# Retention and a bilinear feed-forward on one core: state sums on GpSimd and out of PSUM, marks on ScalarE

## The chip, the cores and the metric

The kernel runs on one core of a Trainium2 chip. A core has TensorE (PE, matrix products into PSUM), VectorE (DVE), ScalarE (ACT), GpSimd (POOL) and SyncE (SP), which here only issues DMAs. Each engine works its own list of instructions in order, and waits where an instruction needs something that another engine or a DMA has yet to deliver. The metric is the time of one execution on the device in microseconds (us); lower is better.

## The reference

```python
gamma = 1.0 - 2.0 ** (-5.0 - np.arange(H))          # B, H, S, D = 4, 8, 768, 64
for t in range(S):
    state = gamma * state + einsum('bhd,bhe->bhde', k[:, :, t], v[:, :, t])
    y[:, :, t] = einsum('bhd,bhde->bhe', q[:, :, t], state) / sqrt(D)
x = y.transpose(0, 2, 1, 3).reshape(B * S, H * D)   # 3072 x 512
out = ((x @ w_a) * (x @ w_b)) @ w_out               # 512 -> 1536 -> 512
```

Inputs and output are float32.

## The kernel before

**Retention.** The 3072 positions are cut into 24 *slots* of 128, six to a batch. The decay is folded into tables that multiply k and q, so a chunk needs scores, a mask and a running state without decay. Slots are worked in *pairs*: pair n is slots n and n + 1. For each slot `casts(t)` (L243) puts on GpSimd two multiplies (`scaled`, L236: k and q by their tables, f32 to bf16, tile kqb) and the cast of v (`cast`, L201, tile vb), and on SyncE the DMA transpose of kqb to kqT (L249). After an odd slot it also issues the loads of the next pair (k, q, then v). So the chain casts, transpose, loads, casts of the next pair runs by itself, as far as buffers allow.

**A visit.** `turn(new, old)` (L407) is called at fixed places, and I name a visit by its arguments: visit 10/8 is `turn(10, 8)`. On TensorE it issues, in this order: the first half of the old pair's products with the state (`inter`, swapped, L369), the new pair's four chunk states in 64 rows (`chunk_states`, L292, two PSUM tiles named st), the new pair's scores (L327), the second half of `inter`, and the products of masked scores with v (`intra`, L381). Between the two halves the rows of a PSUM bank change; a tiny copy, the *mark* (`fenced`, L346), waits for the first half, and the second half waits for the mark.

A state at a chunk's end is the sum of all chunk states up to there. ScalarE copies the two st tiles into the SBUF tile sums (L298); each chunk is then added to the one before it (L303, VectorE, 128x256 f32, both inputs in SBUF), and ScalarE casts the sums to bf16, two at a time (gst, L199), for the next visit's `inter`. The adds are not run at the visit: they go on a list, `unsummed`, and `sum_now` takes one from it in each block of the feed-forward, or all of them behind an output.

**Feed-forward.** The positions form eight *tiles* J of TILES[J] slots (4, 2, 2, 2, 2, 4, 4, 4). Each tile runs twelve *blocks* (`ffn_ab`, L617): a (four matmuls, L594), ScalarE's cast of a to asb (L598), g (four matmuls, L606), VectorE's product of g and asb into ht (L609). In the tiles of FAST, VectorE also adds parts of ht into hsum (L665), and the output is computed for two slots at once by a scheme with seven products in place of eight (`ffn_fast`, L678): ScalarE copies product tiles to snap (L687), VectorE adds snap and PSUM into osb. The products into R1 and R5 go on accumulating after a snap has been taken, so TensorE waits for those copies. The other tiles use `ffn_out` (L632, L642).

**Order.** Each engine's order is the order of the code (`seq`). The dictionary `ahead` (L840) says what runs ahead of which block or output: `(5, 8)` is ahead of block 8 of tile 5, `(5, "o", 2)` ahead of output 2 of tile 5. Small ScalarE work goes on the list `later`: the copies of y to xt, and the casts to gst. `catch_up(n)` takes n from it; a block takes TILES[J] // 2, an `ffn_fast` takes two after its first snap and then one at a time.

The PSUM pool psff is a ring of three banks ("ff"), shared by a, g, o, one of the two st tiles and the fast products. The nat pool holds kqb and vb of six slots, the raw pool the loads of three pairs.

Of the kernel before, what the change touches and what calls it, by code (L numbers as in the profile page):

```python
# [12 lines left out]
ALU = mybir.AluOpType  # L13
# [11 lines left out]
def kernel(  # L25
# [10 lines left out]
    nc = tc.nc  # L36
    P = 128
    B, H, S, D = q.shape
    NCH = S // P
# [32 lines left out]
    def seq(bi):  # L72
        ins = bi.ins
        prev = last.get(ins.engine)
        if prev is not None:
            tc.add_manual_dep(ins, prev.name, nosync, reason="program order")
        last[ins.engine] = ins
        return bi
# [89 lines left out]
    for par in range(2):  # L168
        m = const.tile([P, 1, P], BF16, name=f"mask{par}")
# [8 lines left out]
    gst = const.tile([P, 8, HP, D], BF16, name="gst")  # L178
# [18 lines left out]
    def cast(engine, dst, src):  # L197
        if engine is nc.scalar:
            seq(nc.scalar.copy(dst, src))  # L199
        else:  # L200
            seq(engine.tensor_copy(dst, src))  # L201
# [57 lines left out]
    def half(i):  # L259
        return slice(64 * i, 64 * i + 64)  # L260
# [4 lines left out]
    later = []  # L265

    def catch_up(n=100):
        for fn in later[:n]:
            fn()
        del later[:n]  # L270

    sums = {}

    unsummed = []

    def sum_now(n=100):
        for fn in unsummed[:n]:
            fn()
        del unsummed[:n]

    def chunk_states(n):

        u = [psff.tile([P, 2, HP, D], F32, tag="ff", name="st"),
             psst.tile([P, 2, HP, D], F32, tag="st", name="st")]
        ends = (n + 2) % NCH == 0
        for s in range(2):
            for hp in range(HP):
                for c in range(2):
                    if ends and s and c:
                        continue  # L290
                    for r in range(2):
                        seq(nc.tensor.matmul(u[c][half(r), s, hp, :], kb[n + s][half(c), hp, r, :],  # L292
                                             vb[n + s][half(c), HP * r + hp, :],
                                             start=True, stop=True, skip_group_check=True))
        new = sums[n] = tra.tile([P, 2, 2, HP, D], F32, tag="kqT2", name="sums", bufs=2)
        for c in range(2):
            m = 1 if ends and c else 2
            seq(nc.scalar.copy(new[:, :m, c], u[c][:, :m]))  # L298

        def add_state(s, c):  # L300
            if s or c or n % NCH:
                old = new[:, s, 0] if c else new[:, 0, 1] if s else sums[n - 2][:, 1, 1]
                seq(nc.vector.tensor_tensor(new[:, s, c], new[:, s, c], old, op=ALU.add))  # L303
            m = 1 if ends and s else 2
            if c == m - 1:
                i = (2 * (n + s)) % 8
                later.append(lambda: cast(nc.scalar, gst[:, i : i + m], new[:, s, :m]))

        for s in range(2):
            for c in range(2):  # L310
                if not (ends and s and c):
                    unsummed.append(lambda s=s, c=c: add_state(s, c))

    unmasked = []

    def mask_now(n=100):
        for fn in unmasked[:n]:
            fn()
        del unmasked[:n]

    def scores(n):
        at = psat.tile([P, 2, 2, HP, D], F32, tag="at", name="at")
        for s in range(2):
            for hp in range(HP):
                for c in range(2):
                    for r in range(2):
                        seq(nc.tensor.matmul(at[half(c), r, s, hp, :],  # L327
                                             kqT[n + s][half(r), 0, hp, half(c)],
                                             queries(n + s, r, hp, c),
                                             start=True, stop=True, skip_group_check=True))  # L330
        aT[n] = tra.tile([P, 2, 2, HP, D], BF16, tag="aT", name="aT")
        for r in range(2):
            unmasked.append(lambda r=r: seq(nc.vector.tensor_tensor(  # L333
                aT[n][:, r].rearrange("p s h d -> p (s h) d"),
                at[:, r].rearrange("p s h d -> p (s h) d"),
                mask.to_broadcast([P, 2 * HP, D]), op=ALU.mult)))
# [7 lines left out]
    def fenced(eng):  # L344

        bi = seq(eng.copy(mark, bq) if eng is nc.scalar else eng.tensor_copy(mark, bq))  # L346
        tc.add_manual_dep(bi.ins, last[mybir.EngineType.PE].name, after, reason="rows change banks")
        return bi.ins
# [10 lines left out]
    def inter(o, swap, y):  # L359

        for s in range(2):
            for j in range(2):
                for r in range(2):
                    c = 1 - r if swap else r
                    t = o + s
                    if t % NCH == 0 and c == 0:
                        continue
                    for hp in (2 * j, 2 * j + 1):
                        into(o, c, r, seq(nc.tensor.matmul(  # L369
                            y[c][half(hp % 2), s, 2 * r + j, :], gst[half(r), (2 * t + c - 1) % 8, hp, :],  # L370
                            queries(t, r, hp, c), stop=y is not ys[o],
                            start=y is not ys[o] or begin(o, c, hp % 2),
                            skip_group_check=True)))
# [29 lines left out]
                seq(nc.vector.tensor_tensor(dst[:, s, on], src[:, s, on], part[:, s], op=ALU.add))  # L403
                seq(nc.vector.tensor_copy(dst[:, s, off], src[:, s, off]))

    def turn(new, old, eng=nc.vector):
        sum_now()  # L407
        catch_up()
        apart = None
        if old is not None:  # L410
            ys[old] = [psat.tile([P, 2, KT, D], F32, tag=f"y{c}", name="y") for c in range(2)]
            if new is None:
                both = psat.tile([P, 2, 2, KT, D], F32, tag="at", name="apart")
                apart = [both[:, c] for c in range(2)]
            inter(old, True, ys[old] if new is not None else apart)
            if new is not None:
                fence[old, 0] = fence[old, 1] = fenced(eng)
        if new is not None:
            chunk_states(new)
            scores(new)  # L420
        if old is not None:
            inter(old, False, ys[old])
            intra(old)
            leaves = [lambda c=c: leave(old, c, apart) for c in range(2)]
            later[:] = leaves + later
# [185 lines left out]
    def ffn_ab(J, ft):  # L611
        ffn_a(J, ft)
        ffn_g(J, ft)
        catch_up(TILES[J] // 2)
        sum_now(1)
        mask_now(1)

    held = []
# [118 lines left out]
    D_, G_, A_ = nc.vector, nc.gpsimd, nc.scalar  # L737
# [100 lines left out]
    for j in range(NO):  # L838
        cast_o(j)
    ahead = {  # L840
        (1, 6): [(casts, 6)], (1, 8): [(casts, 7)],
        (0, "o", 2): [(turn, 6, None), (casts, 8, "kq")],
        (0, "o", 3): [(casts, 9, "kq"), (casts, 8, "v"), (casts, 9, "v")],
        (1, "o", 1): [(turn, 8, 6, D_), (casts, 10)],
        (2, 2): [(casts, 11)], (2, 7): [(casts, 12)], (2, "o", 0): [(turn, 10, 8), (casts, 13)],
        (3, 0): [(casts, 14)], (3, 6): [(casts, 15)], (3, "o", 0): [(turn, 12, 10), (casts, 16)],
        (4, 0): [(casts, 17)], (4, 8): [(turn, 14, 12)], (4, "o", 0): [(casts, 18)],
        (4, "o", 1): [(turn, 16, 14, D_), (casts, 19)], (5, 0): [(casts, 20)],
        (5, 2): [(casts, 21)], (5, 8): [(turn, 18, 16), (casts, 22)],
        (5, "o", 2): [(turn, 20, 18, D_), (casts, 23)],  # L850
        (6, 8): [(turn, 22, 20)], (6, "o", 0): [(turn, None, 22)],
    }
    early = {3: [(0, 0, 2)], 4: [(1, 0, 2)], 5: [(2, 0, 2)], 6: [(3, 0, 2)],
# [5 lines left out]
    def visit(*at):  # L859
        for fn, *what in ahead.pop(at, ()):  # L860
            fn(*what)

    def blocks(J):
        for ft in range(NFT):
            if ft > 1 or J == 5:
                store()
            visit(J, ft)
            ffn_ab(J, ft)
            if J in FAST:
                for which, f0, f1 in adds[TILES[J]].get(ft, ()):  # L870
                    add(J, which, f0, f1)
# [3 lines left out]
    for J in range(len(TILES)):  # L875
        if J > 1:
            blocks(J)
        for i in range(TILES[J]):
            visit(J, "o", i)
            if J not in FAST:  # L880
                ffn_out(J, i)
                mask_now(2)
                sum_now()
                if (J, i) in combined:
                    combine_o(*combined[J, i])
            elif i % 2 == 0:
                for which, f0, f1 in adds[TILES[J]].get(NFT, ()):
                    add(J, which, f0, f1)
                ffn_fast(J, i // 2)
# [31 lines left out]
```

## Time and profile before

| | us |
|---|---|
| runs (three): median | 227.32 |
| lowest, highest | 226.63, 232.68 |
| the profiled execution | 226.68 |
| its span on the core | 224.6 |
| span and what lies around it, difference | 2.08 |

In the profile each group or instruction has a line as L609, its engine, what it writes and reads, and its shapes. In a timeline a row is the start, the duration, the engine, the line, the operation, and in brackets how long the engine was idle before it and what ended that.

| where TensorE is, by the trace | us from the span's start |
|---|---|
| visit 10/8, ahead of tile 2's output | 79.62 |
| visit 12/10, ahead of tile 3's output | 97.80 |
| visit 14/12, ahead of block 8 of tile 4 | 111.57 |
| visit 16/14, ahead of tile 4's second output | 120.38 |
| visit 18/16, ahead of block 8 of tile 5 | 138.11 |
| visit 20/18, within tile 5's outputs | 152.32 |
| visit 22/20, ahead of block 8 of tile 6 | 172.04 |

GpSimd's last cast ends at 153.85.

### The profile page before, as it was taken

The numbers are of one execution on the slowest core, as the hardware profiler recorded it, in microseconds if no ns is written. First come the engines' busy times: TensorE is split into PE (matmuls) and PEld (weight loads), VectorE is DVE, ScalarE is ACT, GpSimd is POOL, SyncE is SP. The second block draws the span as 40 slices with busy tenths as digits, with TensorE's granted clock in tenths as the row PEclk, the third lists the DMA queues.
The fourth block names the chain that finished last, engine by engine and source line by source line (L and its number), as shares of the span: only waits on it lengthen the run. The fifth ranks groups of instructions, "written<-read, shape, count | busy, mean of one in ns | idle before, by whom it ended". The sixth has DMA issues, their size and how long they took to land.

```text
span 224.6 us, 6767 instructions
## 1 busy us (share of the span) xinstructions
PE 214.0 (95%) x2803; PEld 149.7 (67%) x2809; DVE 134.8 (60%) x301; ACT 100.7 (45%) x218; POOL 81.7 (36%) x107
## 2 busy tenths in 40 slices
PE   8899999999999979999989998999998999999993
PEld 7578887884458868878865444478544478444582
DVE  2783447559836857765775366693665693356641
ACT  3774353441465344544675533545253543333331
POOL 6557797792642535143453544153000000000000
PEclk9999999999999999999999999999999999999999
DMA  6999999998898995997869898895200002200022
GB/s 184 347 379 382 365 306 392 301 211 180 193 260 191 259 237 94 160 232 196 194 122 235 205 209 218 140 250 146 104 0 3 0 3 93 96 0 0 1 91 99
DMA packets 94831, 39.76 MB, mean 177 GB/s; under 512 B 76113, under 2 KB 91729, under 8 KB 94801
## 3 DMA queue, kind: packets, MB, share of 16 engines
q1 hardware_dynamic: 94656, 39.20, 67.0%
q8 instruction: 22, 0.36, 0.7%
q10 hardware_dynamic: 144, 0.13, 0.2%
q14 instruction: 9, 0.07, 0.1%
HBM read 28.31 MB, written 6.29 MB: 154 GB/s over the span
## 4 chain that ended last, share of the span: by engine, by line
PE 87%; DVE 5%; DMA 3%; issue 2%; POOL 1%; SPq 0%; ACT 0%; DVEq 0%; POOLq 0%; ACTq 0%
PE a L594 27%; PE g L606 27%; PE o L675 17%; PE o L642 9%; DMA kf<-in_k_dram 3%; DVE ht L609 2%; DVE hsum L665 2%; POOL kqb L236 1%; PE y L369 1%; PE y L381 1%; PE at L327 1%; PE tp L452 1%; PE st L292 1%; PE st L493 1%; DVE aT L477 1%
## 5 line engine op out<-in xcount | busy, mean ns | idle before, releaser
L609 DVE TENSOR_TENSOR ht<-g,asb 128x256 bf16<-128x256 f32 (+1 forms) x98 | 53.7, 548 | 52.2 <-PE g L606 48.8
L594 PE MATMUL a<-xt,wa_bf 128*128 128x256 bf16 (+1 forms) x432 | 77.6, 308 | 0.4 <-DVE ht L609 0.2
L606 PE MATMUL g<-xt,wb_bf 128*128 128x256 bf16 (+1 forms) x432 | 77.7, 308 | 0.2 <-DVE ht L609 0.2
L598 ACT CAST asb<-a 128x256 bf16<-128x256 f32 (+1 forms) x98 | 46.2, 472 | 67.7 <-PE a L594 66.9
L606 PEld LDWEIGHTS <-wb_bf 128*128 128x128 bf16 x432 | 42.1, 98 | 20.7 <-issue 0.3
L594 PEld LDWEIGHTS <-wa_bf 128*128 128x128 bf16 x432 | 41.7, 98 | 21.4 <-issue 1.2
L236 POOL TENSOR_TENSOR kqb<-kf,ktab 128x512 bf16<-128x512 f32 x21 | 22.9, 1091 | 36.4 <-DMA kf<-in_k_dram 36.4
L236 POOL TENSOR_TENSOR kqb<-qf,qtab 128x512 bf16<-128x512 f32 x21 | 22.8, 1087 | 9.0 <-DMA qf<-in_q_dram 8.9
L642 PE MATMUL o<-wo_bf,ht 128*128 128x512 bf16 x91 | 21.1, 379 | 1.1 <-ACT asb L598 0.7
L201 POOL CAST vb<-vf 128x512 bf16<-128x512 f32 x24 | 14.9, 630 | 18.6 <-DMA vf<-in_v_dram 12.6
L675 PEld LDWEIGHTS <-hsum 128*128 128x128 bf16 x192 | 18.7, 98 | 2.3
L687 ACT COPY snap<-o 128x256 f32<-128x256 f32 x31 | 11.5, 372 | 17.4 <-PE o L675 15.3
L303 DVE TENSOR_TENSOR sums<-sums 128x256 f32<-128x256 f32 x30 | 17.6, 585 | 0.4
L675 PE MATMUL o<-wt_bf,hsum 128*128 128x256 bf16 x144 | 17.1, 273 | 0.0
L642 PEld LDWEIGHTS <-ht 128*128 128x128 bf16 x96 | 9.2, 98 | 11.2 <-issue 0.9
L675 PEld LDWEIGHTS <-ht 128*128 128x128 bf16 x144 | 13.7, 98 | 2.5 <-DVE ht L609 0.3
L665 DVE TENSOR_TENSOR hsum<-ht 128x256 bf16<-128x256 bf16 (+1 forms) x36 | 12.9, 365 | 0.4
L333 DVE TENSOR_TENSOR aT<-at,mask 128x512 bf16<-128x512 f32 x18 | 12.0, 682 | 1.5 <-PE y L369 0.9
L690 DVE TENSOR_TENSOR osb<-o,snap 128x256 f32<-128x256 f32 x17 | 7.1, 419 | 9.3 <-PE o L675 5.7
L199 ACT CAST gst<-sums 128x512 bf16<-128x512 f32 (+1 forms) x18 | 10.4, 585 | 4.5 <-DVE sums L303 4.3
L675 PE MATMUL o<-wo_bf,ht 128*128 128x256 bf16 x96 | 12.0, 273 | 0.0
L298 ACT COPY sums<-st 128x512 f32<-128x512 f32 (+1 forms) x18 | 9.0, 554 | 4.9 <-PE st L292 4.9
(79 smaller groups left out, 174.6 us busy)
## 6 DMA issues: line engine op xcount, KB each, us to landing
out_dram<-osb SPq DMA_DIRECT2D x11, 512.0 KB, 3.3
kf<-in_k_dram SPq DMA_DIRECT2D x18, 256.0 KB, 3.8
qf<-in_q_dram SPq DMA_DIRECT2D x36, 128.0 KB, 3.9
vf<-in_v_dram SPq DMA_DIRECT2D x18, 256.0 KB, 4.3
wsta<-in_moe_w_a_dram SPq DMA_DIRECT2D x6, 512.0 KB, 7.7
wstb<-in_moe_w_b_dram SPq DMA_DIRECT2D x6, 512.0 KB, 7.8
wsto<-in_moe_w_out_dram SPq DMA_DIRECT2D x6, 512.0 KB, 9.2
kf<-in_k_dram SPq DMA_DIRECT2D x3, 512.0 KB, 5.7
```

The source lines that it names most:

```text
L201: seq(engine.tensor_copy(dst, src))
L236: seq(eng.tensor_tensor(dst, src, tab, op=ALU.mult))
L303: seq(nc.vector.tensor_tensor(new[:, s, c], new[:, s, c], old, op=ALU.add))
L333: unmasked.append(lambda r=r: seq(nc.vector.tensor_tensor(aT[n][:, r].rearrange("p s h d -> p (s h) d"), at[:, r].rearrange("p s h d -> p ...
L594: seq(nc.tensor.matmul(a[:, b0 - c0 : b1 - c0], wa_bf[:, kt, fs], xcols(J, kt, b0, b1), start=(kt == 0 and b0 == c0), stop=(kt == KT - 1 a ...
L598: seq(nc.scalar.copy(asb, a))
L606: seq(nc.tensor.matmul(g[:, b0 - c0 : b1 - c0], wb_bf[:, kt, fs], xcols(J, kt, b0, b1), start=(kt == 0 and b0 == c0), stop=(kt == KT - 1 a ...
L609: seq(nc.vector.tensor_tensor(ht[J][:, ft, c0:c1], g, asbs.pop((J, ft, c0)), op=ALU.mult))
L642: seq(nc.tensor.matmul(o, ht[J][:, ft, i * P : (i + 1) * P], wo_bf[:, f, 2 * r : 2 * r + 2, :].rearrange("p a d -> p (a d)"), start=(ft == ...
L665: seq(nc.vector.tensor_tensor(s[which], x(), y(), op=op))
L675: seq(nc.tensor.matmul(R[:, :DH], lhs, (wo_bf, wt_bf)[w][:, f, m, :], start=(first and f == 0), stop=(f == NH - 1), skip_group_check=True))
L687: seq(nc.scalar.copy(snap[:, i], R[:, :DH]))
```

## The change

The sums of a new pair are now written at its visit, at once, and by the engine given as `adder`. With GpSimd, ScalarE copies the st tiles as before and GpSimd adds in SBUF. With VectorE there is no copy: the add takes st out of PSUM and writes sums. The list `unsummed` and its calls are gone. The mark's engine is ScalarE unless given.

| visit | mark before | mark now | adds now |
|---|---|---|---|
| 6 (no old pair) | none | none | VectorE, PSUM |
| 8/6 | VectorE | VectorE | VectorE, PSUM |
| 10/8, 12/10 | VectorE | ScalarE | GpSimd |
| 14/12 | VectorE | ScalarE | VectorE, PSUM |
| 16/14 | VectorE | VectorE | GpSimd |
| 18/16 | VectorE | ScalarE | GpSimd |
| 20/18 | VectorE | VectorE | GpSimd |
| 22/20 | VectorE | ScalarE | GpSimd |

Of thirty adds nineteen are on GpSimd. On VectorE stand eleven, and one copy for the first state of a batch (visit 6). The casts to gst go on `later` at the visit itself, behind the copies to xt.

```diff
-    def chunk_states(n):
+    def chunk_states(n, eng):
...
         new = sums[n] = tra.tile([P, 2, 2, HP, D], F32, tag="kqT2", name="sums", bufs=2)
-        for c in range(2):
-            m = 1 if ends and c else 2
-            seq(nc.scalar.copy(new[:, :m, c], u[c][:, :m]))
...
+        if eng is nc.gpsimd:
+            for c in range(2):
+                m = 1 if ends and c else 2
+                seq(nc.scalar.copy(new[:, :m, c], u[c][:, :m]))
+        for s in range(2):
             m = 1 if ends and s else 2
...
+            for c in range(m):
+                dst = new[:, s, c]
+                src = dst if eng is nc.gpsimd else u[c][:, s]
+                if s or c or n % NCH:
+                    old = new[:, s, 0] if c else new[:, 0, 1] if s else sums[n - 2][:, 1, 1]
+                    seq(eng.tensor_tensor(dst, src, old, op=ALU.add))
+                elif src is not dst:
+                    seq(eng.tensor_copy(dst, src))
+            i = (2 * (n + s)) % 8
+            later.append(lambda s=s, i=i, m=m: cast(nc.scalar, gst[:, i : i + m], new[:, s, :m]))
...
-    def turn(new, old, eng=nc.vector):
-        sum_now()
+    def turn(new, old, eng=nc.scalar, adder=nc.gpsimd):
...
-            chunk_states(new)
+            chunk_states(new, adder)
...
-        (2, 2): [(casts, 11)], (2, 7): [(casts, 12)], (2, "o", 0): [(turn, 10, 8), (casts, 13)],
+        (2, 2): [(casts, 11)], (2, 7): [(casts, 12, "kq")],
+        (2, "o", 0): [(turn, 10, 8), (casts, 12, "v"), (casts, 13)],
```

The other entries of `ahead` change in the same way: around the visits with sums on GpSimd the cast of v of the slot then at work, and the casts behind it, are written after the visit.

On TensorE and SyncE every instruction stands where it stood. GpSimd at visit 10/8 (kqb: k and q of slot 12, then 13; vb: v of the same), before:

```order
L236 TENSOR_TENSOR kqb<-kf,ktab_735 128x2x4x64
L236 TENSOR_TENSOR kqb<-qf,qtab_736 128x2x4x64
L201 CAST vb<-vf 128x512
L236 TENSOR_TENSOR kqb<-kf,ktab_735 128x2x4x64
L236 TENSOR_TENSOR kqb<-qf,qtab_736 128x2x4x64
```

and now:

```order
L236 TENSOR_TENSOR kqb<-kf,ktab_735 128x2x4x64
L236 TENSOR_TENSOR kqb<-qf,qtab_736 128x2x4x64
L300 TENSOR_TENSOR sums<-sums 128x256 x3
L201 CAST vb<-vf 128x512
L236 TENSOR_TENSOR kqb<-kf,ktab_735 128x2x4x64
L236 TENSOR_TENSOR kqb<-qf,qtab_736 128x2x4x64
```

The three adds stand between q and v of slot 12; the casts keep their order.

ScalarE from visit 12/10 to block 8 of tile 4, before:

```order
L298 COPY sums<-st 128x2x256 x2
L687 COPY snap<-o 128x256
L396 CAST xt<-y 128x2x8x32 x2
L687 COPY snap<-o 128x256 x3
L598 CAST asb<-a 128x256 x3
L199 CAST gst<-sums 128x512
L598 CAST asb<-a 128x256 x2
L199 CAST gst<-sums 128x512
```

and now:

```order
L338 COPY mark<-bq 128x1
L292 COPY sums<-st 128x2x256 x2
L677 COPY snap<-o 128x256
L388 CAST xt<-y 128x2x8x32 x2
L199 CAST gst<-sums 128x512
L677 COPY snap<-o 128x256 x2
L199 CAST gst<-sums 128x512
L677 COPY snap<-o 128x256
L589 CAST asb<-a 128x256 x8
```

The mark is new, and both casts to gst moved from the next tile's blocks into the fast output, among the snap copies. The same holds at 10/8 and 20/18.

VectorE at visit 14/12 (aT is the masked scores; up to block 11 of tile 4), before:

```order
L609 TENSOR_TENSOR ht<-g,asb 128x256 x4
L346 COPY mark<-bq 128x1
L609 TENSOR_TENSOR ht<-g,asb 128x256
L303 TENSOR_TENSOR sums<-sums 128x256
L333 TENSOR_TENSOR aT<-at,mask 128x512
L609 TENSOR_TENSOR ht<-g,asb 128x256
L303 TENSOR_TENSOR sums<-sums 128x256
L333 TENSOR_TENSOR aT<-at,mask 128x512
L609 TENSOR_TENSOR ht<-g,asb 128x256
L303 TENSOR_TENSOR sums<-sums 128x256
L609 TENSOR_TENSOR ht<-g,asb 128x256
L303 TENSOR_TENSOR sums<-sums 128x256
```

and now:

```order
L600 TENSOR_TENSOR ht<-g,asb 128x256 x8
L300 TENSOR_TENSOR sums<-st,sums 128x256 x4
L600 TENSOR_TENSOR ht<-g,asb 128x256
L325 TENSOR_TENSOR aT<-at,mask 128x512
L600 TENSOR_TENSOR ht<-g,asb 128x256
L325 TENSOR_TENSOR aT<-at,mask 128x512
L600 TENSOR_TENSOR ht<-g,asb 128x256 x2
```

The four adds stood behind one ht product each, in blocks 8 to 11; now they read st and stand ahead of block 8's product, and the mark is gone.

More of the change, by code (lines that the diff above doesn't have):

```diff
@@ L272 @@
     sums = {}
[L274 to L279, printed above, removed]
-    def chunk_states(n):
+    def chunk_states(n, eng):
         u = [psff.tile([P, 2, HP, D], F32, tag="ff", name="st"),
@@ L295, in chunk_states @@
         new = sums[n] = tra.tile([P, 2, 2, HP, D], F32, tag="kqT2", name="sums", bufs=2)
-        for c in range(2):
-            m = 1 if ends and c else 2
[L298 to L303, printed above, removed]
-            m = 1 if ends and s else 2
[L305 to L312, printed above, removed]
+        if eng is nc.gpsimd:
[3 more added lines that the diff above has]
+        for s in range(2):
+            m = 1 if ends and s else 2
+            for c in range(m):
[8 more added lines that the diff above has]
+            later.append(lambda s=s, i=i, m=m: cast(nc.scalar, gst[:, i : i + m], new[:, s, :m]))
     unmasked = []
@@ L614, in ffn_ab @@
         catch_up(TILES[J] // 2)
-        sum_now(1)
         mask_now(1)
@@ L841 @@
         (1, 6): [(casts, 6)], (1, 8): [(casts, 7)],
-        (0, "o", 2): [(turn, 6, None), (casts, 8, "kq")],
+        (0, "o", 2): [(turn, 6, None, A_, D_), (casts, 8, "kq")],
         (0, "o", 3): [(casts, 9, "kq"), (casts, 8, "v"), (casts, 9, "v")],
-        (1, "o", 1): [(turn, 8, 6, D_), (casts, 10)],
-        (2, 2): [(casts, 11)], (2, 7): [(casts, 12)], (2, "o", 0): [(turn, 10, 8), (casts, 13)],
[L846 to L850, printed above, removed]
+        (1, "o", 1): [(turn, 8, 6, D_, D_), (casts, 10)],
+        (2, 2): [(casts, 11)], (2, 7): [(casts, 12, "kq")],
+        (2, "o", 0): [(turn, 10, 8), (casts, 12, "v"), (casts, 13)],
+        (3, 0): [(casts, 14, "kq")],
+        (3, "o", 0): [(turn, 12, 10), (casts, 14, "v"), (casts, 15), (casts, 16)],
+        (4, 0): [(casts, 17)], (4, 8): [(turn, 14, 12, A_, D_)],
+        (4, "o", 1): [(turn, 16, 14, D_), (casts, 18), (casts, 19)],
+        (5, 0): [(casts, 20, "kq")],
+        (5, 8): [(turn, 18, 16), (casts, 20, "v"), (casts, 21), (casts, 22, "kq")],
+        (5, "o", 2): [(turn, 20, 18, D_), (casts, 22, "v"), (casts, 23)],
         (6, 8): [(turn, 22, 20)], (6, "o", 0): [(turn, None, 22)],
@@ L882 @@
                 mask_now(2)
-                sum_now()
                 if (J, i) in combined:
```

## The prediction

> **What bounds the kernel now.** I read the page first, then the waits, then TensorE's timeline around each visit, then the engines that it waits for. TensorE is the bound: it is busy for 95% of the span and carries 87% of the chain that ended last; the granted clock is full in every slice. So the change is worth only the gaps that it closes on TensorE.
>
> ```profile
> PE 214.0 (95%) x2803; PEld 149.7 (67%) x2809; DVE 134.8 (60%) x301; ACT 100.7 (45%) x218; POOL 81.7 (36%) x107
> PEclk9999999999999999999999999999999999999999
> PE 87%; DVE 5%; DMA 3%; issue 2%; POOL 1%; SPq 0%; ACT 0%; DVEq 0%; POOLq 0%; ACTq 0%
> ...
> ACT gst L199 <- DVE sums L303: 4.3, 5, 1.2
> PE y L369 <- DVE mark L346: 3.4, 4, 1.3
> PE o L642 <- ACT asb L598: 0.7, 1, 0.7
> ```
>
> In the waits (us in total, times, longest) TensorE stands 3.4 us before the second inter block (L369) until the mark has run. TensorE's timeline says at which visits; the bracket is its idle time:
>
> ```profile
> 81.78 0.32 PE L369 MATMUL y<-kqT,gst 64*64 64x64 bf16 x16 [1.34 <-DVE mark L346]
> 99.17 0.32 PE L369 MATMUL y<-kqT,gst 64*64 64x64 bf16 x16 [0.47 <-DVE mark L346]
> 139.92 0.32 PE L369 MATMUL y<-kqT,gst 64*64 64x64 bf16 x16 [0.92 <-DVE mark L346]
> 173.49 0.32 PE L369 MATMUL y<-kqT,gst 64*64 64x64 bf16 x16 [0.63 <-DVE mark L346]
> ```
>
> These are visits 10/8, 12/10, 18/16 and 22/20 (new pair/old pair), and all four marks go to ScalarE. A second loss is the end of tile 4, behind visit 14/12, where VectorE is overfull:
>
> ```profile
> 112.81 0.61 PE L594 MATMUL a<-xt,wa_bf 128*128 128x256 bf16 x4
> ...
> 117.70 2.75 PE L642 MATMUL o<-wo_bf,ht 128*128 128x512 bf16 x11 [0.71 <-ACT asb L598]
> ...
> 113.97 0.42 DVE L609 TENSOR_TENSOR ht<-g,asb 128x256 bf16<-128x256 f32 x1 [1.73 <-PE g L606]
> 114.31 1.10 DVE L303 TENSOR_TENSOR sums<-sums 128x256 f32<-128x256 f32 x1
> 117.86 0.41 DVE L609 TENSOR_TENSOR ht<-g,asb 128x256 bf16<-128x256 f32 x1
> ```
>
> Four blocks (eight groups of matmuls) take 117.70 - 112.81 = 4.89 us there. A window shows what is normal, and two more show the smaller losses (length, then TensorE's busy time):
>
> ```profile
> 86.91:97.80 10.89, 10.87 (x98) 1.00 0.82 152
> 147.37:152.32 4.95, 4.92 (x43) 1.00 1.08 236
> 153.54:158.14 4.60, 4.60 (x52) 1.00 0.59 171
> ```
>
> Twenty-four groups in 10.89 us are 0.454 each, so eight should take 3.6: 1.3 us are lost. The fast output of tile 5's first half took 4.95 us, its second half 4.60: 0.35 lost.
>
> **The change part by part.** No order changes on TensorE or SyncE, and no DMA is added; GpSimd's casts keep their order too, so that putting v behind a visit does no more than let the adds stand ahead of it. VectorE loses thirty adds and five marks and gains twelve operations out of PSUM; ScalarE loses six copies and gains five marks; GpSimd gains nineteen adds. The prices:
>
> ```profile
> L303 DVE TENSOR_TENSOR sums<-sums 128x256 f32<-128x256 f32 x30 | 17.6, 585 | 0.4
> L690 DVE TENSOR_TENSOR osb<-o,snap 128x256 f32<-128x256 f32 x17 | 7.1, 419 | 9.3 <-PE o L675 5.7 <-ACT snap L687 3.6
> L236 POOL TENSOR_TENSOR kqb<-qf,qtab 128x512 bf16<-128x512 f32 x21 | 22.8, 1087 | 9.0 <-DMA qf<-in_q_dram 8.9
> L199 ACT CAST gst<-sums 128x512 bf16<-128x512 f32 (+1 forms) x18 | 10.4, 585 | 4.5 <-DVE sums L303 4.3
> L298 ACT COPY sums<-st 128x512 f32<-128x512 f32 (+1 forms) x18 | 9.0, 554 | 4.9 <-PE st L292 4.9
> L346 ACT COPY mark<-bq 128x1 f32<-128x1 f32 x2 | 0.4, 191 | 1.0 <-PE y L516 1.0
> ```
>
> *Marks on ScalarE.* A mark costs 0.19 us there. ScalarE has only its asb cast before it and that ends before the first inter block does, so the mark is through while TensorE still runs states and scores. Behind it stand the copies of the states, which wait for that same stretch of TensorE. The four gaps close: 1.34 + 0.47 + 0.92 + 0.63 = 3.36 us gained. What is late next is asked below.
>
> *Sums on VectorE out of PSUM (visits 6, 8, 14).* The nearest row is osb<-o,snap, one PSUM and one SBUF input of the same size: 0.419 us, against 0.585 before. At 14/12 four of them (1.7 us) fall into VectorE's idle 1.73 us before 113.97, and the ScalarE copies go. The ff bank of the states is held until the third add; the ring of three hands it out again one tile-4 block later, about when that add ends, so I take nothing for it (0 to 0.4). The ht products behind lose the four adds between them: I take 1.25 of the 1.3 us. At 6 and 8, 512-wide output matmuls with ScalarE copies hide it: 0.
>
> *Sums off VectorE in the blocks.* Tile 3 had small stalls behind its adds, I take 0.15; the 0.35 us of tile 5 come from a gst cast that waits for a late sum and from late hsum adds, I take 0.3. Together 0.45.
>
> *Sums on GpSimd (visits 10, 12, 16, 18, 20, 22).* The trace has no f32 add on GpSimd. Half of the 512-wide multiply is 0.54 us; were all of it fixed cost it would be 1.09. I take 0.55, nearest to a price by elements, and 0.6 from add to add, since each waits for the one before. The GPSIMD Engine Reference of the Trainium skill (section 4.1, Engine selection) advises VectorE for two-input elementwise work, with GpSimd about 2 times slower; the rows do not bear that out here, since VectorE's SBUF adds average 0.585. By the page's ratio on an uncontended 0.42 us the add would be 0.84, and the sum below 1 us worse by its estimate.
>
> The new wait matters more: a gst cast now stands on ScalarE inside the fast output, and behind it the snap copies that TensorE waits for. At visit 10/8 (GpSimd, then ScalarE):
>
> ```profile
> 80.47 1.04 POOL L236 TENSOR_TENSOR kqb<-kf,ktab 128x512 bf16<-128x512 f32 x1 [4.35 <-DMA kf<-in_k_dram]
> 81.95 1.08 POOL L236 TENSOR_TENSOR kqb<-qf,qtab 128x512 bf16<-128x512 f32 x1 [0.44 <-DMA qf<-in_q_dram]
> 86.47 0.61 POOL L201 CAST vb<-vf 128x512 bf16<-128x512 f32 x1 [3.44 <-PE o L675]
> ...
> 83.49 1.08 ACT L396 CAST xt<-y 128x512 bf16<-128x512 f32 x2
> 84.49 0.37 ACT L687 COPY snap<-o 128x256 f32<-128x256 f32 x1
> 85.14 0.37 ACT L687 COPY snap<-o 128x256 f32<-128x256 f32 x1 [0.28 <-PE o L675]
> 85.80 0.37 ACT L687 COPY snap<-o 128x256 f32<-128x256 f32 x1 [0.28 <-PE o L675]
> ```
>
> The multiplies of slot 12 stand ahead of the sums and wait for DMA, whatever TensorE does, so the sums start at 83.03; the first two are done at 84.2. With the gap closed, ScalarE wants to cast gst at 84.57 - 1.34 = 83.2. It gets there a microsecond late, casts for 0.5, then copies two snaps of 0.3 and 0.37: the second one ends at about 85.4; before it was 85.51. The later product into R1 needs it. So nearly the whole gain of this visit is given back: -1.25.
>
> At 12/10 and 20/18 the sums are in time, but the two gst casts lengthen the run of ScalarE copies, whose slack is 0.28 us a snap: -0.25 each, -0.5. At 18 and 22 they fall into wide blocks with over a microsecond free a block: 0.
>
> *What GpSimd's later work does.* At 10 the adds lie in its idle time before vb (83.03 to 86.47). At 12 they do not:
>
> ```profile
> 98.45 1.07 ACT L298 COPY sums<-st 128x512 f32<-128x512 f32 x2 [0.61 <-PE st L292]
> ...
> 99.63 0.61 POOL L201 CAST vb<-vf 128x512 bf16<-128x512 f32 x1 [2.56 <-PE y L369]
> ...
> 115.15 1.23 SPq L249 DMA_TRANSPOSE kqT<-kqb  x1
> ...
> DMA to landing us min/median/max: 2.8/2.8/2.8
> ...
> 120.77 0.43 PE L327 MATMUL at<-kqT 64*64 64x64 bf16 x29
> ```
>
> The copies would end at 99.52 - 0.3 = 99.2; three adds of 0.6 end at 101.0, and v14 starts 1.4 us later than at 99.63. Slot 15, its transpose, the loads of 16 and 17, their casts and the transpose of 17 all follow in a chain. Queued behind it, that transpose lands at 115.15 + 2.8 + 1.4 = 119.35. Scores of visit 16 reach slot 17 at about 120.9 and would now do so 1.7 us sooner (0.1 + 0.15 + 0.22 + 1.25), at 119.2: TensorE waits 0.2. Visits 18 and 20 have over 2 us to spare.
>
> **The sum.** 3.36 + 1.25 + 0.45 - 1.25 - 0.5 - 0.2 = 3.1 us. The profiled execution took 226.68 us (span 224.6): 223.6. The median of the runs is 227.32, 0.3% above that execution. Two per cent, 4.5 us, is about what a measurement of this kernel can tell from no change.
>
> **The rivals.**
> 1. *No wait on GpSimd bites.* If casts and adds run ahead, the terms -1.25, -0.5 and -0.2 vanish: 5.06 gained, 221.6. For: at 10/8 it takes only q of slot 12 landing 1 us earlier. Against: its load is timed by a DMA chain that this change doesn't shorten.
> 2. *The input chain catches the gains.* Every add that holds v up delays the next loads. With adds of 1.09 us v14 is 2.9 us late and visit 16 stands 1.7 instead of 0.2; 10/8 loses 1 us more. 3.1 - 1.5 - 1.0 = 0.6: 226.1.
> 3. *Slower than before.* At 20/18 the four adds stand behind the multiplies of slot 22, whose loads wait for slot 21, which now waits for the sums of 18. Before (GpSimd, ScalarE):
>
> ```profile
> 147.90 1.11 POOL L236 TENSOR_TENSOR kqb<-qf,qtab 128x512 bf16<-128x512 f32 x1 [0.61 <-DMA qf<-in_q_dram]
> ...
> 154.67 1.08 ACT L396 CAST xt<-y 128x512 bf16<-128x512 f32 x2
> ```
>
> With 1.4 us inherited and 0.9 from the sums of 18 the multiply ends at 149.0 + 2.3 = 151.3, and two adds at 152.5. ScalarE, 2.75 us sooner by then, is ready for gst at 155.75 - 2.75 = 153.0. So the chain has 0.5 us to spare; each microsecond beyond holds gst, then the snaps, then TensorE. From 3.6 us late on, the kernel is slower than before; 5 us late give 228.1. For: GpSimd waited 4.35 us for k at 80.47, so loads are the slow part. Against: nothing but the sums of 18 moves in this chain.
> 4. *The shared port.* The row is hsum, normally 0.28 us, beside GpSimd's multiply at 80.47:
>
> ```profile
> 79.27 0.28 DVE L665 TENSOR_TENSOR hsum<-ht,hsum 128x256 bf16<-128x256 bf16 x1
> ...
> 80.58 1.08 DVE L665 TENSOR_TENSOR hsum<-hsum,ht 128x256 bf16<-128x256 bf16 x1
> ```
>
> It ended with that multiply, 0.8 us late. Six visits with one such hit on the path would cost 4.8 us: 228.4. The hsum adds have over a microsecond before their product at 10 and 12 and no GpSimd add stands beside the ones at 20, so I count none. SBUF — State Buffer of the Trainium skill (Who interferes with whom) calls this an exclusive lock between GpSimd and VectorE operations with two SBUF inputs; the 1.08 agrees, and by it the sums out of PSUM are free of it.
>
> **How the numbers follow.** Forecast 0.58, first rival 0.14, second 0.17, third 0.07, fourth 0.04. The range takes the forecast with its uncertain terms (without the loss at 10/8 it is 222.3) and reaches toward rivals 1 and 2: 221.8 to 226.4. Faster by over 2% is about the first rival, 0.13; slower by over 2% (231.2) needs 3 and 4 together or one much worse, 0.04; the rest 0.83.
>
> **What would show it.** No wait of L369 on a mark; tile 4 ends 3.6 us behind visit 14; GpSimd adds near 0.55 us; at 10/8 a gst cast that waits for GpSimd and products stalled by about a microsecond; a short wait at the scores of visit 16. I am wrong if GpSimd adds take a microsecond, if the slot loads move with the sums, or if gst blocks ScalarE at 20/18.

## The result, and the profile after

| | before | changed |
|---|---|---|
| median of 12 runs each, us | 227.59 | 225.09 |
| lowest, highest | 226.03, 232.68 | 223.73, 230.99 |
| ratio, 95% interval | | 0.9871 (0.9832 to 0.9909) |

The change gains 1.3%, which stays within the bound of 2%, and its time lies inside the predicted range. Medians, here and below, are of all runs, and ratios compare only the runs within 1.5% of their kernel's fastest. The first profile of the changed kernel was taken in a run in which the clock of TensorE fell after a long wait, so a second one, at full clock (`e0_after_again` below, span 222.9 us), is the one read here.

Its groups give the prices of the moved adds (line, engine, operation, shapes, count, then busy time and mean ns of one, then idle time before):

```profile
L300 POOL TENSOR_TENSOR sums<-sums 128x256 f32<-128x256 f32 x19 | 13.8, 726 | 21.3 <-ACT sums L292 18.1 <-issue 2.1
L300 DVE TENSOR_TENSOR sums<-st,sums 128x256 f32<-128x256 f32 x11 | 4.7, 424 | 0.8
```

VectorE's adds out of PSUM cost 0.424 us, 0.419 having been taken; GpSimd's cost 0.726 us, not 0.55. The timeline of TensorE in the same profile:

```profile
80.43 0.32 PE L361 MATMUL y<-kqT,gst 64*64 64x64 bf16 x16
...
86.08 0.82 PE L665 MATMUL o<-wt_bf,hsum 128*128 128x256 bf16 x6 [1.66 <-ACT snap L677]
...
99.49 0.34 PE L361 MATMUL y<-kqT,gst 64*64 64x64 bf16 x16
...
113.33 0.61 PE L585 MATMUL a<-xt,wa_bf 128*128 128x256 bf16 x4
...
116.92 2.75 PE L632 MATMUL o<-wo_bf,ht 128*128 128x512 bf16 x12
...
121.07 0.32 PE L319 MATMUL at<-kqT 64*64 64x64 bf16 x16 [0.77 <-DMA kqT<-kqb]
...
138.99 0.34 PE L361 MATMUL y<-kqT,gst 64*64 64x64 bf16 x16
...
156.66 0.81 PE L665 MATMUL o<-wo_bf,hsum 128*128 128x256 bf16 x6 [0.15 <-ACT snap L677]
...
171.87 0.32 PE L361 MATMUL y<-kqT,gst 64*64 64x64 bf16 x16
```

The rows of the second inter block (L361 is L369 of before) have no bracket any more: the waits for the mark are gone. Tile 4's end takes 116.92 - 113.33 = 3.59 us, against 4.89. Two new waits of some length stand in their place, one on a snap in tile 2's fast output and one on the transpose of slot 17. Read visit by visit, by the start of the second inter block:

| second inter block of visit, us | before | changed (e0) | marks alone (e1) | six out of PSUM (e6) |
|---|---|---|---|---|
| 10/8 | 81.78 | 80.43 | 80.19 | 79.93 |
| 12/10 | 99.17 | 99.49 | 97.51 | 97.27 |
| 16/14 | 121.03 | 121.21 | 119.89 | 117.78 |
| 18/16 | 139.92 | 138.99 | 137.76 | 135.68 |
| 22/20 | 173.49 | 171.87 | 171.52 | 168.20 |
| span | 224.6 | 222.9 | 222.7 | 219.2 |

Up to visit 16/14 the changed kernel has gained nothing (121.21 against 121.03): what the marks and tile 4 brought was spent in tile 2's output, in tile 3 and at 16/14 itself. Its 1.7 us come from behind that point. Each column is one execution. How far two of them can lie apart without any cause in the code is seen in `e4_psum_three` and `e6_psum_six` below: they are the same program up to visit 16/14, and they reach it at 118.13 and 117.13 us. The first profile of the changed kernel shows it too: in tile 2's output TensorE waited 0.80 us on the snap there, and the output took 5.55 us, against 1.66 and 6.42 here.

### The profile page after: what moved, and what is told of

The parts are those of the page before. It is cut to its first block, busy times and chain, and to the rows that moved or that the text cites. A ratio compares the mean times of both kernels' runs of the same rounds, so it can differ in the third digit from the quotient of the medians.

```text
span 226.6 us, 6763 instructions
## 1 busy us (share of the span) xinstructions
PE 214.8 (95%) x2803; PEld 150.4 (66%) x2809; DVE 122.4 (54%) x278; ACT 98.5 (43%) x217; POOL 94.5 (42%) x126
## 4 chain that ended last, share of the span: by engine, by line
PE 70%; DMA 11%; SPq 6%; POOL 5%; issue 3%; ACT 2%; DVE 1%; POOLq 0%; DVEq 0%
PE a L585 23%; PE g L597 22%; PE o L665 13%; PE o L632 5%; DMA kf<-in_k_dram 5%; DMA vf<-in_v_dram 3%; SPq L93 3%; POOL kqb L236 3%; DMA kqT<-kqb 2%; POOL sums L300 2%; SPq L95 2%; DMA qf<-in_q_dram 2%; PE y L361 1%; PE y L373 1%; PE st L285 1%
## 5 line engine op out<-in xcount | busy, mean ns | idle before, releaser
L300 POOL TENSOR_TENSOR sums<-sums 128x256 f32<-128x256 f32 x19 | 13.8, 724 | 24.3 <-ACT sums L292 22.1
L632 PE MATMUL o<-wo_bf,ht 128*128 128x512 bf16 x91 | 21.9, 389 | 0.5 <-issue 0.3
L709 DVE TENSOR_TENSOR osb<-o,snap 128x512 f32<-128x512 f32 x7 | 4.8, 692 | 11.7 <-PE o L665 9.7
```

Source lines behind the costliest of these rows:

```text
L300: seq(eng.tensor_tensor(dst, src, old, op=ALU.add))
L632: seq(nc.tensor.matmul(o, ht[J][:, ft, i * P : (i + 1) * P], wo_bf[:, f, 2 * r : 2 * r + 2, :].rearrange("p a d -> p (a d)"), start=(ft == ...
```

## The experiments

Each was timed beside the kernel before, whose median was 227.14 us beside e0 to e3 and 227.44 us beside e4 to e7.

**The changed kernel again, and one part alone.** `e0_after_again` is the changed kernel as it stands.

> The changed kernel once more, on the chip of the next three, for a profile at full clock. My theory: 3.1 us gained by the prediction's terms, ratio 0.986; a wait of 0.8 to 1.3 us inside the fast output of tile 2, a wait at the scores of visit 16/14 whose length follows the loads of slots 16 and 17 (0.2 us by the prediction, 3.66 us in the profile shown), and none before L361 for a mark. The rival, that the wait at 16/14 is a fixed part of the change: 3 us or more of it in this profile too.

Median 226.01 us (224.77 of the runs that count for the ratio), ratio 0.9895 (0.9853 to 0.9937). The wait at 16/14 was 0.77 us here and 3.66 us in the first profile, so its length is no fixed part of the change. Of the 2.9 us between, 1.0 is that TensorE came to the visit sooner there (118.64 against 119.60), and 1.8 that the transpose landed later. In tile 2's output TensorE waited 1.66 us, more than I said. `e1_marks_only` changes a single word of the kernel before:

```diff
-    def turn(new, old, eng=nc.vector):
+    def turn(new, old, eng=nc.scalar):
```

> The kernel before with nothing changed but the five marks on ScalarE; sums stay on VectorE. My theory: the four waits before the second inter block (3.36 us) close and the fast outputs carry no gst cast, so nothing is given back: about 3.3 us gained, ratio 0.985, tile 4's end still 1.3 us long, no wait at 16/14 beyond 0.3 us. The rival: the mark only shows how late VectorE is, and the first product after it (R1 needs ht, later hsum) waits in its place: under 1 us gained, ratio above 0.996.

Median 223.36 us, ratio 0.9822 (0.9774 to 0.987). By the runs the marks alone gain 1.8% or 4 us, where 3.36 had been predicted for them; that is at least what the whole change gains (the median is below its 224.77, the intervals overlap). That nothing takes up the wait in its place, though, the trace does not show. It was taken in the slowest of the six runs (224.45 us). In it the stretches from the visit to the second inter block shrink by 3.99 us in all at the four visits, but the span by 1.9 only, since TensorE loses time behind them: tile 3's blocks take 11.46 us against 10.89, the first eight blocks of tile 4 7.88 against 7.26, and tile 5's first fast output 5.91 against 4.95. So in this execution the rival is half right. The two longest waits, the first of which the prediction had read off before:

```profile
116.46 2.75 PE L642 MATMUL o<-wo_bf,ht 128*128 128x512 bf16 x12 [0.71 <-ACT asb L598]
...
148.97 1.59 PE L675 MATMUL o<-wt_bf,hsum 128*128 128x256 bf16 x13 [1.06 <-DVE hsum L665]
```

The first is tile 4's end, the second tile 5's first fast output. There hsum stands behind the sums of visit 18, but the order alone does not make it late. VectorE and GpSimd in the same trace:

```profile
146.12 1.22 DVE L303 TENSOR_TENSOR sums<-sums 128x256 f32<-128x256 f32 x1
...
147.45 1.14 DVE L665 TENSOR_TENSOR hsum<-ht 128x256 bf16<-128x256 bf16 x1
...
146.00 1.04 POOL L236 TENSOR_TENSOR kqb<-kf,ktab 128x512 bf16<-128x512 f32 x1 [4.86 <-DMA kf<-in_k_dram]
147.40 1.04 POOL L236 TENSOR_TENSOR kqb<-qf,qtab 128x512 bf16<-128x512 f32 x1 [0.35 <-DMA qf<-in_q_dram]
```

The add and one hsum, which alone take 0.41 and 0.28 us in this trace, started just behind a multiply of GpSimd and ended only after it. This is the row of the prediction's fourth rival. In e4 below the order there is the same, the multiplies start at 147.49, behind that add, the add takes 0.41 us, and the output 4.95 us with no such wait.

**The change without its marks.** `e2_marks_back`:

```diff
-    def turn(new, old, eng=nc.scalar, adder=nc.gpsimd):
+    def turn(new, old, eng=nc.vector, adder=nc.gpsimd):
...
-        (4, 8): [(turn, 14, 12, A_, D_)],
+        (4, 8): [(turn, 14, 12, D_, D_)],
```

> The changed kernel with all its marks on VectorE again; the sums stay where the change put them. My theory: taking the adds off VectorE does not clear its queue at the mark, since ht and hsum stand there: waits of about 1.3, 0.5, 0.9 and 0.6 us before L361 come back; at 10/8 the loss in the fast output falls away in exchange, so about 2 us worse than the changed kernel, ratio to the kernel before about 0.995. The rival: with the adds gone the marks are early on VectorE too, and the time is that of the changed kernel, 0.986.

Median 225.90 us, ratio 0.997 (0.9941 to 0.9999). In TensorE's timeline the waits are back:

```profile
82.35 0.32 PE L361 MATMUL y<-kqT,gst 64*64 64x64 bf16 x16 [1.27 <-DVE mark L338]
...
86.60 0.82 PE L665 MATMUL o<-wt_bf,hsum 128*128 128x256 bf16 x6 [0.27 <-ACT snap L677]
...
100.34 0.32 PE L361 MATMUL y<-kqT,gst 64*64 64x64 bf16 x16 [0.47 <-DVE mark L338]
...
140.19 0.32 PE L361 MATMUL y<-kqT,gst 64*64 64x64 bf16 x16 [1.00 <-DVE mark L338]
```

They are as long as before (1.34, 0.47, 0.92; the fourth, at 22/20, is 0.63 in both), though VectorE no longer adds the sums: ht and hsum ahead of the mark set it. The snap wait at 10/8 shrank from 1.66 to 0.27, as the exchange demands. So with the marks left on VectorE the sums' new places are worth 0.3%, and most of the change's gain is that of the marks.

**Where the gain of the marks goes: the loads.** `e3_sums12_vector` takes the three adds of visit 12/10 off GpSimd:

```diff
-        (3, "o", 0): [(turn, 12, 10), (casts, 14, "v"), ...],
+        (3, "o", 0): [(turn, 12, 10, A_, D_), (casts, 14, "v"), ...],
```

> The changed kernel with only the sums of visit 12/10 moved to VectorE, out of PSUM. My theory: the cast of v14 no longer stands behind three GpSimd adds, so slot 15, the loads of 16 and 17 and the transpose of 17 come about 2 us sooner and the wait at the scores of 16/14 is gone; up to 0.8 us is lost in tile 3's fast output, where R4 needs the bank that the third add frees. Ratio to the changed kernel between 1.000 and 0.993. The rival: the loads of 16 and 17 are late by themselves (DMA), the wait at 16/14 stays as in the changed kernel.

Median 224.09 us, ratio 0.9865 (0.9819 to 0.9912), which can't be told from the changed kernel, but the trace answers the question. In the changed kernel (e0), GpSimd and SyncE:

```profile
100.48 2.34 POOL L300 TENSOR_TENSOR sums<-sums 128x256 f32<-128x256 f32 x3 [4.17 <-ACT sums L292]
102.77 0.61 POOL L201 CAST vb<-vf 128x512 bf16<-128x512 f32 x1
...
115.63 0.61 POOL L201 CAST vb<-vf 128x512 bf16<-128x512 f32 x1 [2.09 <-DMA vf<-in_v_dram]
...
118.27 1.23 SPq L249 DMA_TRANSPOSE kqT<-kqb  x1
```

The adds end at 102.8, v14 starts 3.1 us later than before (99.63), and 13 us on, v16 still stands 3.1 us later (112.51 before, from the same view), and slot 17's transpose too (118.27 against 115.15). In e3, GpSimd, VectorE, TensorE:

```profile
111.84 0.61 POOL L201 CAST vb<-vf 128x512 bf16<-128x512 f32 x1 [3.79 <-DMA vf<-in_v_dram]
...
98.45 0.91 DVE L655 TENSOR_TENSOR hsum<-ht 128x256 bf16<-128x256 bf16 x1
99.40 1.01 DVE L655 TENSOR_TENSOR hsum<-hsum,ht 128x256 bf16<-128x256 bf16 x1
...
100.85 1.34 DVE L300 TENSOR_TENSOR sums<-st,sums 128x256 f32<-128x256 f32 x3
...
101.79 0.83 PE L665 MATMUL o<-wt_bf,ht 128*128 128x256 bf16 x6 [1.21 <-DVE sums L300]
```

v16 is 3.8 us sooner and no wait at 16/14 is left. The adds are paid at another place: they hold the bank that the third fast product needs, for 1.21 us, the more so as two hsum adds ran 0.9 and 1.0 us beside GpSimd's multiplies of slot 15 (98.18 to 100.27), in place of 0.28. So here adds out of PSUM cost ahead of a fast output what they gained at the loads.

**The gst cast in the fast output.** `e5_gst_later` keeps the casts of visits 10, 12 and 20 back:

```diff
-            later.append(lambda s=s, i=i, m=m: cast(...))
+            (kept if n in (10, 12, 20) else later).append(lambda s=s, i=i, m=m: cast(...))
...
     def blocks(J):
+        later.extend(kept)
+        kept.clear()
```

> The changed kernel with the casts to gst of visits 10, 12 and 20 kept back until the next tile's blocks; sums on GpSimd as in the change. My theory: the waits of TensorE on snap (1.66 us at 10/8, 0.15 at 20/18, about 0.2 more in slowed products) come from the gst cast alone and fall away; about 1.5 us of that reach the end, since at 16/14 the wait for the transpose of slot 17 grows by part of what is gained. Ratio to the kernel before 0.983, wait at 16/14 1.5 us or more. The rival: snaps wait for ScalarE's other copies, nothing moves, 0.989.

Median 227.30 us; in five of its six runs the mean granted clock was 0.985 to 0.992, so there is no ratio, and the one at full clock took 222.37 us. TensorE's timeline has no wait on a snap up to visit 22, so those waits did come from the gst cast. What was gained there reappeared at 16/14, more than I expected:

```profile
122.79 0.32 PE L320 MATMUL at<-kqT 64*64 64x64 bf16 x16 [3.50 <-DMA kqT<-kqb]
```

The visit began 1.6 us sooner than in e0 (117.97 against 119.60), but v16 was cast at 115.62 as in e0 (115.63), and the transpose of 17, issued at 118.26 as in e0 (118.27), took 4.5 us to land in place of 2.8. A gain ahead of a visit whose input is late is no gain.

**The order of v.** `e7_v_ahead` is the changed kernel with the casts where they stood before:

```diff
-        (2, 2): [(casts, 11)], (2, 7): [(casts, 12, "kq")],
-        (2, "o", 0): [(turn, 10, 8), (casts, 12, "v"), (casts, 13)],
+        (2, 2): [(casts, 11)], (2, 7): [(casts, 12)], (2, "o", 0): [(turn, 10, 8), (casts, 13)],
...
```

> The changed kernel with its casts at the places of the kernel before, so the sums stand behind v and the later slots' casts on GpSimd. My theory: at 10/8 the sums start only when v12 has landed and is cast, about 3.5 us later than in the changed kernel, and gst, the snaps and TensorE with them: 3 us or more lost there, and at 12/10 and 18/16 the sums stand behind a further slot: ratio 1.005 or above. The rival: the order of v matters little, since loads set GpSimd's pace: 0.989.

Median 230.22 us, ratio 1.0106 (1.0063 to 1.0148). At 10/8, GpSimd, ScalarE, TensorE:

```profile
85.30 0.61 POOL L201 CAST vb<-vf 128x512 bf16<-128x512 f32 x1 [3.29 <-DMA vf<-in_v_dram]
85.87 2.33 POOL L300 TENSOR_TENSOR sums<-sums 128x256 f32<-128x256 f32 x3
...
87.42 0.62 ACT L199 CAST gst<-sums 128x512 bf16<-128x512 f32 x1 [4.04 <-POOL sums L300]
...
88.64 1.15 PE L665 MATMUL o<-wt_bf,hsum 128*128 128x256 bf16 x6 [4.07 <-ACT snap L677]
```

v12's load, then the adds, then gst, then the snap, then TensorE: 4.07 us. The rows are the chain of the new wait at its full length. It comes back behind 16/14, where I had not expected it (TensorE, GpSimd, ScalarE):

```profile
131.87 1.02 PE L585 MATMUL a<-xt,wa_bf 128*128 128x512 bf16 x4 [2.83 <-ACT osb L635]
...
128.57 2.32 POOL L300 TENSOR_TENSOR sums<-sums 128x256 f32<-128x256 f32 x3
...
130.13 0.62 ACT L199 CAST gst<-sums 128x512 bf16<-128x512 f32 x1 [4.34 <-POOL sums L300]
...
131.24 0.58 ACT L635 COPY osb<-o 128x512 f32<-128x512 f32 x1
```

There a copy of the output out of PSUM stands behind gst, and tile 5's next a waits for its bank. Putting v behind the visits is what makes adds on GpSimd bearable; it isn't a gain by itself.

**Without GpSimd.** `e4_psum_three` and `e6_psum_six` start from the kernel before with marks on ScalarE, and take the sums of some visits out of PSUM at once; the others stay on VectorE in SBUF, in the blocks.

```diff
+        direct = n in (6, 8, 14)          # e6: (6, 8, 14, 16, 18, 22)
+        if not direct:
...
+            src = u[c][:, s] if direct else new[:, s, c]
...
+        if direct:
+            sum_now()
```

> Marks on ScalarE, and the sums of visits 6, 8 and 14 on VectorE out of PSUM as in the change; the other six visits' sums on VectorE in SBUF, a block at a time, as before; nothing on GpSimd. My theory: the gain of the marks alone (3.4 to 4 us) plus the 1.25 us at the end of tile 4: ratio 0.977, wait of 1.06 us before L675 in tile 5's fast output stays. The rival: tile 4's end is bound by ScalarE as much as by VectorE, and the ratio is that of the marks alone, 0.982.

Median 222.71 us, ratio 0.9801 (0.9758 to 0.9843). From the second inter block of visit 14 to tile 4's output it takes 115.45 - 111.40 = 4.05 us, against 116.46 - 111.26 = 5.20 with the marks alone (rows of the same view): 1.15 us gained there, about what was predicted for it. The two medians differ by 0.65 us, and the intervals overlap; the timing alone doesn't settle it. That the wait of 1.06 us in tile 5 stays was wrong: it isn't there, for the reason given at e1.

```profile
111.40 0.31 PE L376 MATMUL y<-kqT,gst 64*64 64x64 bf16 x11
...
115.45 2.75 PE L649 MATMUL o<-wo_bf,ht 128*128 128x512 bf16 x11
```

> As the kernel with three visits out of PSUM, with visits 16, 18 and 22 out of PSUM too (VectorE idles there for 1.1 us or more behind the states); 10, 12 and 20, whose fast output needs the bank soon, keep SBUF sums in the blocks. My theory: tile 5's first fast output no longer waits for late hsum (1.06 us): 221 us, ratio 0.972. The rival: the adds ahead of mask and mark make VectorE late at another place, ratio 0.977 or above.

Median 222.09 us, ratio 0.9767 (0.9718 to 0.9815), the lowest of all: 2.3% below the kernel before and, in the table above, ahead of the changed kernel at every visit. My figure was 0.972 and the rival's 0.977, so the rival's is nearer, and the interval holds both. My reason is a small part at most: tile 5's first fast output takes 4.68 us, against 4.95 in e4, where there was no wait of 1.06 to remove. Nor does the time tell e6 from e4 (222.71), as the intervals overlap; of the 1.7 us between their spans 1.0 stands ahead of visit 16/14, where the two are one program. In e6's profile TensorE is busy for 97% of the span and its timeline shows no wait above 0.2 us between visits 8 and 22, though tile 3's blocks still take 11.48 us against 10.89 before:

```profile
PE 212.7 (97%) x2803; PEld 149.5 (68%) x2809; DVE 132.9 (61%) x298; ACT 96.4 (44%) x211; POOL 81.2 (37%) x107
```

VectorE is as busy as before the change (61% against 60%). So it isn't less work on VectorE that gained here, but which of its instructions TensorE has to wait for.

## Why the prediction was right

The forecast was 3.1 us gained; the ratio of 0.9871 is 2.9 us of 226.68, that of e0 (0.9895) 2.4, and the profile at full clock shows 1.7. By its terms (e0 against the profile before; a positive number is a gain):

| term | predicted | measured | |
|---|---|---|---|
| marks on ScalarE | 3.36 | 3.96 | the inter blocks of 10, 12, 18, 22 begin 0.65 to 0.81 us after the visit, before 1.37 to 2.16 |
| tile 4's end | 1.25 | 1.30 | 4.89 to 3.59 |
| blocks and tile 5's first output | 0.45 | -0.12 | the output 4.95 to 4.67; tile 3's blocks 10.89 to 11.29 |
| tile 2's output at 10/8 | -1.25 | -1.82 | 4.60 to 6.42 |
| tile 3's and 5's outputs | -0.5 | -0.52 | 4.60 to 4.77 and 4.95 |
| visit 16/14 | -0.2 | -0.7 | TensorE's stretch from visit to output, 1.45 to 2.16 |

The sum of the measured column is 2.1 us; 0.2 us later at the first visit and small differences make it 1.7. Every term but one has its sign; that the time came out near the forecast is in part luck: the marks gained 0.6 us more than said, all the losses together cost 1.1 us more, and the blocks 0.6. And each entry is of one execution: the loss at 10/8 is 1.82 us here and 0.95 in the first profile (5.55 against 4.60), on both sides of the 1.25 predicted.

*Marks.* The mechanism is shown from both sides: alone they give 0.9822, and with all else changed but not them the waits return at their old length. The stretch from the visit to the second inter block shrank by 3.96 us, 0.6 more than the four gaps. The bracket counts from the end of the matmul before, and where nothing waits the next one begins some 0.17 us ahead of that end (in e0 at 80.43, the scores before it ending at 80.17 + 0.43).

*Out of PSUM.* 0.424 us against 0.419; at 14/12 it was free, as said. That an add in SBUF costs 0.585 was a misreading: the row is a mean. In the kernel before half of these adds took 0.42 us or less and the longest 1.25, and all that took over 0.6 overlap a multiply of GpSimd.

*GpSimd's adds.* The step at fault is "I take 0.55": 0.726 us was measured, between the ends given (0.54 and 1.09), and 0.80 us from add to add, not 0.6. At 10/8 (e0: GpSimd, then ScalarE) the path is the one predicted; two adds are done 0.65 us later than said (84.2), 0.37 by their price and 0.28 because the multiplies ended later:

```profile
82.30 1.04 POOL L236 TENSOR_TENSOR kqb<-qf,qtab 128x512 bf16<-128x512 f32 x1
83.31 2.33 POOL L300 TENSOR_TENSOR sums<-sums 128x256 f32<-128x256 f32 x3
...
84.87 0.62 ACT L199 CAST gst<-sums 128x512 bf16<-128x512 f32 x1 [1.63 <-POOL sums L300]
85.39 0.64 ACT L677 COPY snap<-o 128x256 f32<-128x256 f32 x2
```

The multiplies end at 83.3, two adds at 84.83, and ScalarE, idle for 1.63 us, casts gst and only then copies the snaps. The Trainium skill's factor of about 2 (GPSIMD Engine Reference, Engine selection) would, as an estimate, have put the add at 0.84; with 0.726 against VectorE's 0.42 the runs show 1.7. It was nearer than half of the multiply. As for its advice, the three variants without adds on GpSimd have the lowest medians (e1, e4, e6), but what cost most in the others was the place of the adds ahead of loads and snaps; the one run of e5 at full clock (222.37 us) has them on GpSimd too.

*The loads.* "v14 starts 1.4 us later" was mis-sized too: 3.1 us. Of the 1.7 us between, 0.5 are the adds' price; the rest is that visit 12/10 came 1.2 us later than the sum had it (98.68 against 97.5), because 10/8 had given its gain back and more and tile 3's blocks took 0.4 us longer. That the delay would pass on whole through slot 15, the loads and the casts to slot 17 was right: 3.1 us at v14, v16 and the transpose. One of the prediction's own signs of being wrong, loads that move with the sums, is thus there, though its sum held 1.4 us of it.

*Rivals.* The first didn't occur: all three losses were there. The second (the input chain catches the gains) is partly what happened at 16/14, where v14 was as late as it says (3.1 us, it has 2.9), and e5 shows it in full. The third didn't occur in e0: at 20/18 the adds were in time and TensorE lost 0.35 us in that output. Its beginning is in the first profile, where the second gst cast there waited 0.44 us for GpSimd's sums and the output took 5.33 us, 0.73 more than before. The fourth was too lightly dismissed: it is behind e1's 1.06 us, e3 shows two hsum adds lengthened by 0.6 and 0.7 us in the path, and tile 3's 0.4 us in e0 are of that kind too (VectorE, GpSimd, TensorE):

```profile
94.30 1.11 DVE L655 TENSOR_TENSOR hsum<-ht,hsum 128x256 bf16<-128x256 bf16 x1
95.33 0.41 DVE L600 TENSOR_TENSOR ht<-g,asb 128x256 bf16<-128x256 f32 x1
...
94.22 1.04 POOL L236 TENSOR_TENSOR kqb<-kf,ktab 128x512 bf16<-128x512 f32 x1 [4.94 <-DMA kf<-in_k_dram]
95.22 1.09 POOL L236 TENSOR_TENSOR kqb<-qf,qtab 128x512 bf16<-128x512 f32 x1
...
95.80 0.60 PE L585 MATMUL a<-xt,wa_bf 128*128 128x256 bf16 x4 [0.20 <-DVE ht L600]
```

The multiplies were there before the change as well; which VectorE instruction they hit depends on when their loads land.

## What to carry to other kernels

Where an engine waits for a tiny instruction, move that instruction to a queue that has nothing ahead of it, and measure this alone before moving the work that made the first queue late: here the small move alone gained at least as much as the whole change. Before placing work on an idle engine, look at what its queue feeds: GpSimd's idle time lay between loads, and each add in it delayed a chain of cast, transpose and load that comes back to TensorE two visits later. Where no one needs its bank soon, a sum may leave PSUM directly: out of SBUF the add was no slower by itself (0.41 us), but a multiply on GpSimd could make it three times as long. Before a gain of a microsecond in one trace is believed, compare a stretch in which the two kernels are the same.

## What the runs showed of the hardware

Long waits of TensorE were followed by a lower clock. In the first profile of the changed kernel TensorE stood 3.66 us at 16/14; the windows around it (length, TensorE's busy time, granted clock, DMA share, GB/s):

```profile
112.00:118.00 6.00, 5.95 (x87) 1.00 1.23 164
118.00:124.00 6.00, 2.34 (x124) 0.88 0.64 144
124.00:130.00 6.00, 5.67 (x31) 0.84 1.01 266
130.00:134.00 4.00, 4.00 (x20) 1.00 0.61 125
```

In e5, behind 3.50 us, the window from 124 to 130 us has a clock of 0.74:

```profile
124.00:130.00 6.00, 6.00 (x22) 0.74 1.16 280
```

and in e7, behind 4.07 us, the one from 88 to 92 us has 0.62:

```profile
88.00:92.00 4.00, 3.36 (x18) 0.62 0.17 39
```

Around the waits of 1.66 and 0.77 us in e0 the clock stayed at 1.00; for the first:

```profile
80.00:90.00 10.00, 8.32 (x183) 1.00 0.71 153
```

So a wait at 16/14 that grows to some 3.5 us slows the matmuls behind it for a few us as well. The Trainium skill (TensorE: Matmul & The Clock Gate, Part 1) states that the clock is throttled after an idle window of about 3.4 us; the windows agree. Over a whole run the mean granted clock was 0.993 or less in six of the twelve runs of e0, five of the six of e5, all twelve of e7 and one of six of e6, and in none of the thirty of e1 to e4 and one of the forty of the kernel before. That a long wait is behind it in the runs without a trace is likely, not shown.

Beside a multiply of GpSimd a VectorE add with both inputs in SBUF took up to 1.25 us in place of 0.41 (before), and an hsum add up to 1.14 in place of 0.28 (e1). The adds with one input in PSUM took 0.417 to 0.426 us in every case in e0, e4 and e6.

Why the transpose of slot 17 took 2.8 us to land in e0 and 4.6 in the first profile, from the same place in the queue, stays open. In e0 and e5, which issue it within 0.01 us of each other, the DMA traffic is alike, some 290 GB/s from 119.4 to 120.4, which by its place is this transpose, and still it landed 1.7 us later in e5. So the traffic alone does not explain it.
